# Two attention-decode blocks with their output projections: output weights loaded in rows of 4 KB and 2 KB, head outputs put in that order by selection matmuls

## The chip, the cores and the metric

The kernel runs on one core of one Trainium2 chip. The metric is the device time of one execution in microseconds (us). A core has five engines that run side by side and wait for each other through semaphores: TensorE (PE in the profile, with its weight loads as PEld), VectorE (DVE), ScalarE (ACT), GpSimd (POOL) and SyncE (SP), which here only issues loads. The loads themselves are moved by 16 DMA engines.

## The reference: what is computed

Two attention layers decode one new token for a batch of 4. Each has 32 query heads of 128 elements and a model width of 512. All data is bfloat16.

```python
q = (x @ wq)                                  # [4, 512] @ [512, 4096]
scores = einsum("bhqd,bhkd->bhqk", q, k) * (128 ** -0.5)
p = softmax(scores, axis=-1)
o = einsum("bhqk,bhkd->bhqd", p, v)           # [4, 32, 1, 128]
y = o.reshape(4, 1, 32 * 128) @ wo            # [4, 4096] @ [4096, 512]
```

- Part A, the sliding block: 8 key/value heads, each shared by 4 query heads, and only the last 2048 of 8192 cached positions.
- Part B, the block-cached part: 32 key/value heads and all 8192 positions.

The two results are put side by side: the output is [4, 1, 1024]. Nearly all the data is the caches of part B: 4 x 32 x 8192 x 128 x 2 bytes for the keys and as much for the values, 537 MB of the 587 MB that the kernel reads. The output weights `A_wo` and `B_wo` are 4 MB each.

## The kernel before, in words

**Chunks.** The work is cut into 72 chunks. Chunks 0 to 7 are part A: one key/value head with its 4 query heads for all 4 batch rows, 2 MB of keys and 2 MB of values. Chunks 8 to 71 are part B: one pair of heads and one batch row, 4 MB of keys and 4 MB of values, so four chunks to a pair of heads. A chunk is 64 (A) or 128 (B) tiles of 128 cached positions, handled in groups of 8, numbered g.

**One chunk.** `keys_part` (line 650) runs, for each group g, 8 transposes of key tiles on TensorE (`emit_T`, they land in the PSUM tile `tr`), a copy of the result to SBUF by VectorE or ScalarE (`kt`, lines 437 and 439), and, two groups behind, 8 score matmuls (`emit_S`, PSUM tile `sc`). `values_part` (line 672) runs the value matmuls of the chunk before (`emit_pv`, PSUM tile `po`), between them the last scores of the new chunk, then its maximum and exponential (`stats_rowmax`, `stats_gmax`, `stats_exp`). `norm_sum` makes the sums of the softmax by a matmul with ones, and `norm_out` (line 605) multiplies `po` by their inverse and writes the head outputs, `oT` for part A and `oz` for part B. `emit_fin` (line 618) multiplies head outputs by output weights and adds into one PSUM bank, `fin`, over all chunks.

**The output weights.** `dma_wo(g)` (line 304) loads the 4 heads of a part A group, `dma_wos(hp)` (line 311) the 2 heads of a part B pair. Partition d of the destination takes element d of every head: 4 or 2 separate rows of 512 elements, 1 KB each. The stationary operand of an output matmul is then one head's column of `oT` or `oz`, 128 partitions by 4 batch rows, as `norm_out` left it. Part A makes 4 such matmuls a chunk, part B 2 for every two chunks.

**Order.** Nothing is scheduled by a tool: every engine runs its instructions in the order in which the program adds them (`_Sched.add`), and a wait blocks all that stands behind it on that engine. The calls that matter here stand in `keys_part`:

```python
if 1 <= c < NCA and g == 3:
    stats_exp(c - 1)
if 1 <= c < NCA and g == 6:
    norm_sum(c - 1)
if 2 <= c < NCA and g == 4:
    emit_fin(c - 2)
...
if c >= NCA and c % 2 == 1 and g == 10:
    emit_fin(ahead(c, 2))
```

`finish_A` (line 698) ends part A: for its last chunk it runs statistics, sums, values and output matmuls one after the other. After the last chunk of part B come `norm_sum`, the value matmuls and `emit_fin` (lines 722 to 726).

**Loads.** All big loads are issued by SP in one fixed order (lines 352 to 367). A load waits until its buffer is free: keys until the last transposes of the chunk two before, values until the value matmuls of the chunk two before, output weights of part A until `emit_fin` of the chunk two before, those of part B until the last `emit_fin` of the pair before. SP issues in order, so a load that waits holds back all behind it. `sch.mark` (line 653) marks two-chunk stretches; stretches that repeat become hardware loops on TensorE, VectorE and ScalarE.

Of the kernel before, what the change touches and what calls it, by code (L numbers as in the profile page):

```python
# [19 lines left out]
NSM = 2  # L20
# [2 lines left out]
LASTV = (64, 32, 16, 16)  # L23

TRM0, BC0, L0, Q0, XT0 = 0, 256, 288, 320, 448


class _Record:
# [129 lines left out]
def bass_concat_heads__sliding_block_cached__mha_block_cached__decode_kernel(  # L158
        nc, A_x, A_k, A_v, A_wq, A_wo, B_x, B_k, B_v, B_wq, B_wo, out):
    NB = A_x.shape[0]  # L160
# [4 lines left out]
    DO = A_wo.shape[1]  # L165
    W = min(4096, max(256, SkA // 4))
    REP = HQ // Hkv
# [21 lines left out]
    NC = len(chunks)  # L189
    NCA = Hkv  # L190
# [11 lines left out]
    NONE = -1  # L202
    sch = _Sched()
    with ExitStack() as es:
        block = es.enter_context(nc.Block())

        def sb(name, shape, dt):
            return es.enter_context(nc.sbuf_tensor(name, shape, dt))

        def ps(name, shape, dt):  # L210
            return es.enter_context(nc.psum_tensor(name, shape, dt))
# [26 lines left out]
        oT = sb("oT", [P, NSM, 16], BF16)  # L238
        oz = sb("oz", [P, 8], BF16)
        outsb = sb("outsb", [36, DO], BF16)  # L240
        tr = ps("tr", [P, NTRB, TG * P], BF16)
        sc = ps("sc", [P, 2, 512], F32)
        po = ps("po", [P, 512], F32)
# [30 lines left out]
        sch.add("pool", lambda e: e.memset(pbt[1][:, :, :], 0.0), key=("c_pb", 1))  # L274


        half_of = {}
        held = [[] for _ in range(NH)]
        HALF_A = {"k": (8, 9), "v": (4, 5)}
# [21 lines left out]
        def wo_slot(g):  # L301
            return g % 2 if g < NCA - 1 else 2

        def dma_wo(g):
            src = A_wo[g * 4 * P:(g + 1) * 4 * P, :].rearrange("(hl d) n -> d hl n", d=P)
            slot = wo_slot(g)
            dst = wor[:, slot, :].rearrange("p (hl n) -> p hl n", hl=4)
            sch.add_dma("sp", lambda e: e.dma_start(dst, src), "d_wo%d" % slot,
                        waits=[("fin", g - 2)] if g >= 2 and slot < 2 else [], key=("wo", g))

        def dma_wos(hp):

            src = B_wo[2 * hp * P:2 * (hp + 1) * P, :].rearrange("(hl d) n -> d hl n", d=P)
            sch.add_dma("sp", lambda e: e.dma_start(wos[:, :, :], src), "d_wos",  # L314
                        waits=[("fin", NCA + 4 * hp - 1)] if hp else [], key=("wos", hp))

        def dma_kv(kind, c):
# [51 lines left out]
        ms_read = []  # L369
# [3 lines left out]
        def pe_mm(o, l, r, start=True, stop=True, transpose=False, waits=(), key=None):  # L373
            if transpose:
                sch.add("pe", lambda e: e.transpose(o, l, r), waits, key)  # L375
            else:
                sch.add("pe", lambda e: e.matmul(o, l, r, start=start, stop=stop), waits, key)  # L377
# [229 lines left out]
        def norm_out(c):  # L607
            if 0 <= c < NCA:
                m = c % NSM
                o, i0, i1 = oT[:, m, :], po[:, m * 16:m * 16 + 16], rinv[:, m, :]  # L610
            else:

                o, i0 = oz[:, :].rearrange("p (x y) -> p x y", x=2), bcast(po[:, 0:4], [[0, 2], [1, 4]])
                i1 = rz[:, :].rearrange("p (x y) -> p x y", x=2)
            waits = [("rinv" if 0 <= c < NCA else "rz", c), ("pv", c)] + ([("fin", c - 2 if c != NCA + 1 else NONE)] if c >= 2 else [])
            sch.add("dve", lambda e: e.tensor_tensor(out=o, in0=i0, in1=i1, op=ALU.mult), waits=waits, key=("oT", c))  # L616
            po_read[:] = [("oT", c)]

        def emit_fin(c):
# [103 lines left out]
        for g in range(chunks[NC - 1]["NG"]):  # L723
            emit_pv(NC - 1, g)
        pv_done(NC - 1)
# [60 lines left out]
```

## Time and profile before

| What | Value |
|---|---|
| Median of 3 runs | 1381.89 us (1379.97 to 1385.78) |
| Profiled execution: its own time | 1380.14 us |
| Profiled execution: span of the profile | 1378.3 us |
| TensorE busy | 1174.6 us, 85% of the span |
| VectorE busy | 641.7 us, 47% |
| ScalarE busy | 436.0 us, 32% |
| GpSimd busy | 4.8 us |
| Bytes moved | 587.53 MB, mean 426 GB/s over the span |
| DMA packets | 30085 |
| Output matmuls, part A (`fin<-wor,oT`) | 32 |
| Output matmuls, part B (`fin<-wos,oz`) | 66 |

How to read it: the span is what the profiler saw of one execution, from the first to the last instruction, and the execution's own time is a little longer. The page cuts the span into 40 slices of 34.5 us and gives for each the busy share of every engine and of the 16 DMA engines in tenths, where 9 means 90% or more. A share of busy time says nothing yet of what sets the end: part A fills about the first 125 us of the span, part B the rest, and the two have different limits. A line of the timeline gives start, duration, engine, line and operation, output and inputs, and in brackets how long the engine stood idle before it and what it waited for. The "landing" of a load is the time from its issue on SP until its last byte is there. Loads on one queue land in the order of issue, so the difference between the landing of the load before and the issue of the next is the work that the DMA engines still had in hand.

### The profile page before, as it was taken

How to read it: one execution, taken by the hardware profiler on the slowest of the kernel's cores; microseconds unless marked ns; L12 is line 12 of the kernel's file. 1: busy time of each engine (PE TensorE's matmuls, PEld its weight loads, DVE VectorE, ACT ScalarE, POOL GpSimd, SP SyncE). 2: the span in 40 equal slices, each digit the busy share in tenths (PEclk: the TensorE clock that was granted, in tenths of full speed). 3: DMA queues.
4: the chain of work that ended last, by engine and by line, in shares of the span. 5: the costliest groups of instructions: out<-in, count | busy, mean ns of one | idle time of the engine just before them, and what ended most of it. 6: DMA issues, size and time to landing. Idle time of an engine off the chain costs nothing.

```text
span 1378.3 us, 59408 instructions
## 1 busy us (share of the span) xinstructions
PE 1174.6 (85%) x26901; PEld 1132.8 (82%) x26901; DVE 641.7 (47%) x1337; ACT 436.0 (32%) x649; POOL 4.8 (0%) x18
## 2 busy tenths in 40 slices
PE   4887898888888888888889888988898888888988
PEld 4776898888888887888888888888898888888987
DVE  1665454444444444444444444444454445444543
ACT  1553233323223322332233232322333233332332
POOL 1000000000000000000000000000000000000000
PEclk9999999999999999999999999999999999999998
DMA  9999999999999999999999999999999999999997
GB/s 400 414 417 425 428 432 429 431 432 430 433 430 434 428 432 431 431 432 430 432 429 433 431 432 432 430 430 432 431 431 433 428 433 432 431 431 431 430 431 315
DMA packets 30085, 587.53 MB, mean 426 GB/s; under 512 B 2784, under 2 KB 10992, under 8 KB 11248
## 3 DMA queue, kind: packets, MB, share of 16 engines
q1 hardware_dynamic: 30040, 587.22, 99.6%
q8 instruction: 16, 0.26, 0.1%
q14 instruction: 5, 0.04, 0.0%
q10 hardware_dynamic: 24, 0.01, 0.0%
HBM read 587.21 MB, written 0.01 MB: 426 GB/s over the span
## 4 chain that ended last, share of the span: by engine, by line
DMA 60%; PE 37%; DVE 1%; issue 1%; ACT 0%; SPq 0%; DVEq 0%; ACTq 0%
DMA kv<-in_B_k_cache_dram 58%; PE tr L375 23%; PE sc L377 10%; PE po L377 3%; DMA kv<-in_B_wq_dram 2%; PE fin L377 2%; PE ms L377 1%; DVE sA L488 1%; DVE kt L439 0%; DVE sA L486 0%; ACT pba L551 0%; PE ms L375 0%; SPq L330 0%; SPq L314 0%; ACT kt L437 0%
## 5 line engine op out<-in xcount | busy, mean ns | idle before, releaser
L375 PE MATMUL tr<-identb,kv 128*128 128x128 bf16 x8704 | 703.5, 232 | 160.6 <-DMA kv<-in_B_k_cache_dram 158.2
L439 DVE COPY kt<-tr 128x1024 bf16<-128x1024 bf16 x736 | 503.5, 691 | 469.6 <-PE tr L375 468.6
L375 PEld LDWEIGHTS tr<-identb,kv 128*128 128x128 bf16 x8704 | 559.2, 105 | 185.7 <-DMA kv<-in_B_k_cache_dram 103.5
L437 ACT ACTIVATE kt<-tr 128x1024 bf16<-128x1024 bf16 x352 | 360.2, 1024 | 629.8 <-PE tr L375 628.9
L377 PE MATMUL sc<-qb,kt 128*128 128x64 bf16 x8704 | 446.9, 196 | 10.6 <-DVE kt L439 10.3
L377 PEld LDWEIGHTS sc<-qb,kt 128*128 128x128 bf16 x8704 | 369.3, 100 | 14.5 <-DVE kt L439 11.6
L377 PE MATMUL po<-pbb,kv 128*128 128x64 bf16 (+1 forms) x8320 | 293.8, 191 | 7.0 <-issue 7.0
L377 PEld LDWEIGHTS po<-pbb,kv 128*128 128x128 bf16 x8320 | 266.8, 97 | 9.1 <-issue 7.3
L536 ACT ACTIVATE pbb<-sc,negb 64x128 bf16<-64x128 f32 x128 | 51.2, 400 | 295.2 <-DVE negb L526 294.4
L502 DVE TENSOR_REDUCE rm<-sc 64x1 f32<-64x128 f32 x128 | 37.0, 289 | 93.1 <-PE sc L377 92.2
L514 DVE TENSOR_REDUCE gm<-ms 1x2 f32<-1x128 f32 (+1 forms) x72 | 20.1, 279 | 44.5 <-PE ms L375 44.4
L526 DVE COPY negb<-ms 128x1 f32<-128x1 f32 (+1 forms) x72 | 11.4, 159 | 55.4 <-PE ms L377 55.4
L377 PE MATMUL ms<-identf,gx 1*128 1x1 f32 (+1 forms) x144 | 27.2, 256 | 0.0
L377 PEld LDWEIGHTS ms<-identf,gx 1*128 1x128 f32 (+1 forms) x144 | 21.1, 182 | 4.5 <-DVE gx L518 0.4
L536 ACT ACTIVATION_READ_ACCUMULATOR pbb<-sc,negb 64x1 f32 x128 | 23.7, 185 | 0.0
L375 PE MATMUL ms<-identf,rm 128*1 128x128 f32 (+1 forms) x72 | 19.5, 271 | 2.3 <-DVE rm L497 2.3
L377 PE MATMUL po<-pba,kv 128*128 128x64 bf16 x512 | 20.1, 199 | 0.5 <-ACT pba L551 0.5
L377 PE MATMUL fin<-wos,oz 128*4 128x512 bf16 x66 | 20.0, 385 | 0.3 <-DVE oz L616 0.3
L377 PEld LDWEIGHTS po<-pba,kv 128*128 128x128 bf16 x512 | 17.9, 102 | 0.6 <-ACT pba L551 0.6
L518 DVE TENSOR_SCALAR gx<-gm 1x128 f32<-1x128 f32 (+1 forms) x72 | 15.9, 221 | 2.7 <-DVE gm L514 0.2
L377 PE MATMUL ms<-xT,kv 128*128 128x4 bf16 x256 | 7.1, 166 | 8.5 <-DMA kv<-in_A_wq_dram 4.4
L377 PEld LDWEIGHTS ms<-xT,kv 128*128 128x128 bf16 x256 | 7.0, 104 | 8.7 <-DMA kv<-in_A_wq_dram 4.5
(46 smaller groups left out, 136.0 us busy)
## 6 DMA issues: line engine op xcount, KB each, us to landing
kv<-in_B_k_cache_dram SPq DMA_DIRECT2D x64, 4096.0 KB, 27.3
kv<-in_B_v_cache_dram SPq DMA_DIRECT2D x63, 4096.0 KB, 32.0
kv<-in_A_k_cache_dram SPq DMA_DIRECT2D x8, 2048.0 KB, 14.0
kv<-in_A_v_cache_dram SPq DMA_DIRECT2D x8, 2048.0 KB, 16.2
kv<-in_A_wq_dram SPq DMA_DIRECT2D x1, 4096.0 KB, 12.3
kv<-in_B_wq_dram SPq DMA_DIRECT2D x1, 4096.0 KB, 27.2
wor<-in_A_wo_dram SPq DMA_DIRECT2D x8, 512.0 KB, 11.3
wos<-in_B_wo_dram SPq DMA_DIRECT2D x16, 256.0 KB, 20.8
```

The costliest lines, as they stand in the source:

```text
L375: sch.add("pe", lambda e: e.transpose(o, l, r), waits, key)
L377: sch.add("pe", lambda e: e.matmul(o, l, r, start=start, stop=stop), waits, key)
L437: sch.add("act", lambda e: e.activation(dst, src, ACTF.Copy), waits=waits, key=("ev", s))
L439: sch.add("dve", lambda e: e.tensor_copy(dst, src), waits=waits, key=("ev", s))
L488: emit = lambda e, src=src, b=b: e.scalar_tensor_tensor(out=t, in0=src, scalar=mk[:, b:b + 1], in1=t, op0=ALU.mult, op1=ALU.add)
L502: sch.add("dve", lambda e, src=src, pp=pp: e.tensor_reduce(out=rm[pp, m, 0:1], in_=src, axis=AX.X, op=ALU.max), waits=[("S", ch["s_last"]) ...
L514: sch.add("dve", lambda e: e.tensor_reduce(out=gm[0:C, m, 0:U], in_=src, axis=AX.X, op=ALU.max), waits=[("trm", c)], key=("gmax", c))
L518: sch.add("dve", lambda e: e.tensor_scalar(out=dst, in0=gv, scalar1=-scale, scalar2=None, op0=ALU.mult), waits=[("gmax", c)], key=("gx", c))
L526: sch.add("dve", lambda e: e.tensor_copy(negb[:, m, 0:C], ms[:, col:col + C]), waits=[("bc", c)], key=("negb", c))
L536: sch.add("act", lambda e, src=src, pp=pp, n=n, u=u: e.activation(pbv[pp, :, u], src, ACTF.Exp, bias=negb[pp, m, 0:1], scale=scale, accum_ ...
```

## The change

The rows in which the output weights lie in memory are taken as they come: partition p takes 4 (part A) or 2 (part B) neighbouring rows of the weight matrix, which are one piece of 4 KB or 2 KB. Partition p then no longer holds element p of each head, so the head outputs must be put in the same order before the output matmul. Ten 0/1 matrices made by GpSimd at the start serve for that: `sel4` and `sel2` pick elements, `back2` puts part B weights back in head order.

- `emit_sel(c)` is new: 4 (A) or 2 (B) selection matmuls of a 128x128 0/1 matrix with the head outputs (16 or 8 columns) into the PSUM tile `ms`, then 4 or 2 VectorE copies, each of 32 or 64 partitions, into `zA` or `zB`. `emit_fin` takes its stationary operand from there, and waits for the last copy.
- In `keys_part` of part A, `emit_sel` takes the place of `emit_fin` at g=4, and `emit_fin` moves to g=7. In part B `emit_sel` is added at g=8, and `emit_fin` stays at g=10.
- `norm_out` waits for the selection of the chunk two before and no longer for its output matmuls. What next writes to `ms` (the sums, the maximum) waits for the last copy.
- In `finish_A`, `emit_sel(NCA - 2)` is added after the maximum, `emit_fin(NCA - 2)` moves behind `stats_exp`, and `emit_sel(NCA - 1)` stands between the values and the last output matmuls of part A.
- For the last two chunks of part B the weights are put back in head order instead: `emit_wol` adds 4 matmuls of 512 columns and two copies (ScalarE and VectorE) between the last `norm_sum` and the last value matmuls.
- The matmul that clears `fin` waits for the 0/1 matrices.

```diff
+        for r in range(4):
+            sch.add("pool", lambda e, r=r: e.affine_select(
+                out=sel4[:, r, :], in_=onesb[:, :], pattern=[[0, 4], [-4, 32]], compare_op=ALU.is_equal,
+                fill=0.0, base=-r, channel_multiplier=1), waits=["c_onesb"])
...
         def dma_wo(g):
-            src = A_wo[g * 4 * P:(g + 1) * 4 * P, :].rearrange("(hl d) n -> d hl n", d=P)
+            src = A_wo[g * 4 * P:(g + 1) * 4 * P, :].rearrange("(p r) n -> p (r n)", r=4)
...
         def dma_wos(hp):
-            src = B_wo[2 * hp * P:2 * (hp + 1) * P, :].rearrange("(hl d) n -> d hl n", d=P)
+            src = B_wo[2 * hp * P:2 * (hp + 1) * P, :].rearrange("(p r) n -> p (r n)", r=2)
...
-            waits = [("rinv" if 0 <= c < NCA else "rz", c), ("pv", c)] + ([("fin", c - 2 if c != NCA + 1 else NONE)] if c >= 2 else [])
+            waits = [("rinv" if 0 <= c < NCA else "rz", c), ("pv", c)] + ([("sm", c - 2 if c != NCA + 1 else NONE)] if c >= 2 else [])
...
+        def emit_sel(c):
+            if 0 <= c < NCA:
+                sel, x, n, z, k = sel4, oT[:, c % NSM, :], 16, zA[:, c % 2, :], 4
+                free = [("fin", c - 2)] if c >= 2 else []
+            else:
+                sel, x, n, z, k = sel2, oz[:, :], 8, zB[:, :], 2
+                free = [("fin", c - 2 if c - 2 >= NCA else NONE)] if c != NONE else []
+            for r in range(k):
+                pe_mm(ms[:, Z0 + r * n:Z0 + (r + 1) * n], sel[:, r, :], x,
+                      waits=[("oT", c)] + ms_read if r == 0 else [], key=("sm", c) if r == k - 1 else None)
+            for h in range(k):
+                pp = slice(h * P // k, (h + 1) * P // k)
+                src = ms[pp, Z0:Z0 + k * n].rearrange("p (r b h) -> p h r b", r=k, b=NB)[:, h]
+                sch.add("dve", lambda e, src=src, pp=pp: e.tensor_copy(z[pp, :].rearrange("p (r b) -> p r b", r=k), src),
+                        waits=[("sm", c)] + free if h == 0 else [], key=("z", c) if h == k - 1 else None)
+            ms_read[:] = [("z", c)]
+
+        def emit_wol():
+            for u in range(2):
+                o = tr[:, u, :].bitcast(F32)
+                for r in range(2):
+                    pe_mm(o, back2[:, u, r, :], wos[:, r, :], start=r == 0, stop=r == 1,
+                          waits=[("wos2", NC - 1)] if u == r == 0 else [], key=("back", u) if r else None)
+                if u == 0:
+                    sch.add("act", lambda e, o=o: e.activation(wol[:, 0, :], o, ACTF.Copy), waits=[("back", 0)], key=("wol", 0))
+                else:
+                    sch.add("dve", lambda e, o=o: e.tensor_copy(wol[:, 1, :], o), waits=[("back", 1)], key=("wol", 1))
...
-            if ab == 1:
+            if c == NC - 1:
                 ov = oz[:, :].rearrange("p (b u) -> p b u", u=2)
-                ops = [(ov[:, :, u], wos[:, u, :]) for u in range(2)]
-                waits = [("oT", c), ("wos2", c)]
+                ops = [(ov[:, :, u], wol[:, u, :]) for u in range(2)]
+                waits = [("oT", c), ("wol", 0), ("wol", 1)]
+            elif ab == 1:
+                ops = [(zB[:, r * NB:(r + 1) * NB], wos[:, r, :]) for r in range(2)]
+                waits = [("z", c), ("wos2", c)]
             else:
-                w = wor[:, wo_slot(c), :].rearrange("p (hl n) -> p hl n", hl=4)
-                ov = oT[:, c % NSM, :].rearrange("p (u c) -> p u c", c=REP)
-                ops = [(ov[:, :, cc], w[:, cc, :]) for cc in range(REP)]
-                waits = [("oT", c), ("wo", c)]
+                w = wor[:, wo_slot(c), :].rearrange("p (r n) -> p r n", r=4)
+                ops = [(zA[:, c % 2, r * NB:(r + 1) * NB], w[:, r, :]) for r in range(4)]
+                waits = [("z", c), ("wo", c)]
...
                 if 2 <= c < NCA and g == 4:
+                    emit_sel(c - 2)
+                if 2 <= c < NCA and g == 7:
                     emit_fin(c - 2)
...
+                if c >= NCA and c % 2 == 1 and g == 8:
+                    emit_sel(ahead(c, 2))
                 if c >= NCA and c % 2 == 1 and g == 10:
                     emit_fin(ahead(c, 2))
...
         def finish_A():
             stats_gmax(NCA - 1)
+            emit_sel(NCA - 2)
+            stats_exp(NCA - 1)
             emit_fin(NCA - 2)
-            stats_exp(NCA - 1)
             norm_sum(NCA - 1)
             for g in range(chunks[NCA - 1]["NG"]):
                 emit_pv(NCA - 1, g)
             pv_done(NCA - 1)
+            emit_sel(NCA - 1)
             emit_fin(NCA - 1)
...
-                pe_mm(fin[0:36, :], pbt[0][:, 1, 0:36], pbt[0][:, 1, 0:DO], stop=False, waits=[("c_pb", 1)])
+                pe_mm(fin[0:36, :], pbt[0][:, 1, 0:36], pbt[0][:, 1, 0:DO], stop=False, waits=["c_sel"])
...
         norm_sum(NC - 1)
+        emit_wol()
         for g in range(chunks[NC - 1]["NG"]):
             emit_pv(NC - 1, g)
```

More of the change, by code (lines that the diff above doesn't have):

```diff
@@ L25 @@
 TRM0, BC0, L0, Q0, XT0 = 0, 256, 288, 320, 448
+Z0 = Q0
 class _Record:
@@ L240, in bass_concat_heads__sliding_block_cached__mha_block_cached__decode_kernel @@
         outsb = sb("outsb", [36, DO], BF16)
+        sel4 = sb("sel4", [P, 4, P], BF16)
+        sel2 = sb("sel2", [P, 2, P], BF16)
+        back2 = sb("back2", [P, 2, 2, P], BF16)
+        zA = sb("zA", [P, 2, 16], BF16)
+        zB = sb("zB", [P, 8], BF16)
+        wol = sb("wol", [P, 2, DO], BF16)
         tr = ps("tr", [P, NTRB, TG * P], BF16)
@@ L274, in bass_concat_heads__sliding_block_cached__mha_block_cached__decode_kernel @@
         sch.add("pool", lambda e: e.memset(pbt[1][:, :, :], 0.0), key=("c_pb", 1))
+        for r in range(4):
[3 more added lines that the diff above has]
+        for r in range(2):
+            sch.add("pool", lambda e, r=r: e.affine_select(
+                out=sel2[:, r, :], in_=onesb[:, :], pattern=[[0, 2], [-2, 64]], compare_op=ALU.is_equal,
+                fill=0.0, base=-r, channel_multiplier=1))
+            for u in range(2):
+                sch.add("pool", lambda e, r=r, u=u: e.affine_select(
+                    out=back2[:, u, r, :], in_=onesb[:, :], pattern=[[1, P]], compare_op=ALU.is_equal,
+                    fill=0.0, base=P * u - r, channel_multiplier=-2), key="c_sel" if r == u == 1 else None)
         half_of = {}
@@ L304, in dma_wo @@
         def dma_wo(g):
-            src = A_wo[g * 4 * P:(g + 1) * 4 * P, :].rearrange("(hl d) n -> d hl n", d=P)
+            src = A_wo[g * 4 * P:(g + 1) * 4 * P, :].rearrange("(p r) n -> p (r n)", r=4)
             slot = wo_slot(g)
-            dst = wor[:, slot, :].rearrange("p (hl n) -> p hl n", hl=4)
+            dst = wor[:, slot, :]
             sch.add_dma("sp", lambda e: e.dma_start(dst, src), "d_wo%d" % slot,
@@ L311, in dma_wos @@
         def dma_wos(hp):
-            src = B_wo[2 * hp * P:2 * (hp + 1) * P, :].rearrange("(hl d) n -> d hl n", d=P)
-            sch.add_dma("sp", lambda e: e.dma_start(wos[:, :, :], src), "d_wos",
+            src = B_wo[2 * hp * P:2 * (hp + 1) * P, :].rearrange("(p r) n -> p (r n)", r=2)
+            sch.add_dma("sp", lambda e: e.dma_start(wos[:, :, :].rearrange("p r n -> p (r n)"), src), "d_wos",
                         waits=[("fin", NCA + 4 * hp - 1)] if hp else [], key=("wos", hp))
@@ L614, in norm_out @@
                 i1 = rz[:, :].rearrange("p (x y) -> p x y", x=2)
-            waits = [("rinv" if 0 <= c < NCA else "rz", c), ("pv", c)] + ([("fin", c - 2 if c != NCA + 1 else NONE)] if c >= 2 else [])
+            waits = [("rinv" if 0 <= c < NCA else "rz", c), ("pv", c)] + ([("sm", c - 2 if c != NCA + 1 else NONE)] if c >= 2 else [])
             sch.add("dve", lambda e: e.tensor_tensor(out=o, in0=i0, in1=i1, op=ALU.mult), waits=waits, key=("oT", c))
             po_read[:] = [("oT", c)]
+        def emit_sel(c):
[15 more added lines that the diff above has]
+        def emit_wol():
+            for u in range(2):
+                o = tr[:, u, :].bitcast(F32)
+                for r in range(2):
+                    pe_mm(o, back2[:, u, r, :], wos[:, r, :], start=r == 0, stop=r == 1,
[4 more added lines that the diff above has]
+                    sch.add("dve", lambda e, o=o: e.tensor_copy(wol[:, 1, :], o), waits=[("back", 1)], key=("wol", 1))
         def emit_fin(c):
```

## The prediction

> **What bounds the kernel now.** I read the page's slices and chain first, then the waits, then each load's landing, then the timeline of one sliding-block chunk and of the end.
>
> ```profile
> DMA  9999999999999999999999999999999999999997
> DMA packets 30085, 587.53 MB, mean 426 GB/s; under 512 B 2784, under 2 KB 10992, under 8 KB 11248
> DMA 60%; PE 37%; DVE 1%; issue 1%; ACT 0%; SPq 0%; DVEq 0%; ACTq 0%
> wor<-in_A_wo_dram SPq DMA_DIRECT2D x8, 512.0 KB, 11.3
> wos<-in_B_wo_dram SPq DMA_DIRECT2D x16, 256.0 KB, 20.8
> ```
>
> The 16 DMA engines are busy in every slice. 8192 of the packets are the 1 KB rows of the output weights. In the waits of all engines, TensorE stands still mostly for keys of the block-cached part:
>
> ```profile
> PE tr L375 <- DMA kv<-in_B_k_cache_dram: 158.2, 59, 4.5
> PE po L377 <- issue: 7.0, 3, 3.2
> ```
>
> So that part, from about 225 us on, runs at the pace of the transfers, with 158.2/59 = 2.7 us of slack for TensorE per chunk. The sliding-block part does not: its chain of waits between 36 and 104 us holds only TensorE, VectorE and ScalarE pieces. One of its chunks, from the timeline:
>
> ```profile
> 107.02 1.03 PE L377 MATMUL fin<-wor,oT 128*4 128x512 bf16 x4
> 107.45 1.71 ACT L551 ACTIVATE pba<-eA,mk 128x256 bf16<-128x256 bf16 x4
> 107.98 0.62 PE L375 MATMUL tr<-identb,kv 128*128 128x128 bf16 x8
> 108.00 0.69 DVE L439 COPY kt<-tr 128x1024 bf16<-128x1024 bf16 x1
> 109.06 2.17 ACT L437 ACTIVATE kt<-tr 128x1024 bf16<-128x1024 bf16 x2
> 110.12 0.41 PE L377 MATMUL sc<-qb,kt 128*128 128x64 bf16 x8
> 110.36 0.86 PE L377 MATMUL po<-pba,kv 128*128 128x64 bf16 x24
> 112.40 0.48 DVE L486 TENSOR_SCALAR sA<-sc,mk 128x256 f32<-128x256 f32 x1 [2.24 <-PE sc L377]
> ```
>
> The scores at 110.12 wait for ScalarE's first copy (109.06 + 1.02), which is behind the four copies of the probabilities. The output matmuls at 107.02 lie inside that wait. What covers a late load is the queue: the landing of each load, asked around its issue, e.g. of the last sliding-block value load:
>
> ```profile
> L330 SPq DMA_DIRECT2D kv<-in_A_v_cache_dram x1: 541/541/541, 101.7 to 101.7; - x1
> ...
> DMA to landing us min/median/max: 11.5/11.5/11.5
> ```
>
> It lands at 113.2, 4.9 us behind the load before it (108.3). So when it was issued (101.72) the queue still held 6.6 us of work. By the same reading the next loads found 12.4 us (issue 123.20), 10.2 (135.95), 10.7 (145.12), 8.0 (157.56), 9.2 (166.04), 7.1 (177.88), 11.8 (182.85), 10.7 (193.73), and 14 to 23 from 209 on.
>
> **What the Trainium skill says.** "DMA: Bandwidth & Descriptors", section Why small descriptors are slow (HBM only): each packet carries a fixed overhead of about 3 cycles beside its 32-byte beats; its Specifications name 512 B as the least size for line rate. The trace agrees that 1 KB rows are nearly at rate: 46 ns each (below). The same page, Anatomy of one DMA, gives about 2.0 us of fixed cost per DMA (on GpSimd's path); here the last output DMA, issued at 1376.53 on SP, ends by 1378.3, 1.8 us. I use 2.0 us for a load that finds the queue empty. "Runtime: NRT & Kernel Launch", section Instruction fetch mechanics: TensorE holds 2048 instructions, fetched in blocks of 256. The built loop bodies grow from 818 to 838 and from 1594 to 1599 instructions, so both still fit; the trace shows 16 fetched packets in all, 0.26 MB, no refetching.
>
> **The change part by part.**
>
> *Rows of the weights.* Each DMA engine takes 1/16. A 4 MB load lands 9.72 us behind the last one: 8 packets of 32 KB, 1215 ns each. A sliding-block weight load lands 1.45 us after (32 packets of 1 KB, 45 ns), a block-cached one 0.74 (16, 46 ns). The line through 1 KB and 32 KB is 37.7 ns per KB + 8.3 ns per packet. So 4 KB costs 159 ns and 2 KB 84 ns: a sliding-block load 8 x 159 = 1.27 against 32 x 46 = 1.47 us, -0.20; a block-cached one 8 x 84 = 0.67 against 0.74, -0.07. In all 8 x 0.20 + 16 x 0.07 = 2.7 us. Bounds: 0 if the cost goes by bytes. At most the whole excess: landings of successive keys are 39.63 us apart with a weight load between them and 38.83 without, so 0.80 where 0.61 is the full rate, 0.19 x 16 = 3.0; a sliding-block trio takes 11.33 where 10.93 is the rate, 0.40 x 8 = 3.2; together 6.2.
>
> *Sliding-block output matmuls, from g=4 to g=7.* Selection takes their place at g=4: 4 matmuls with 16 columns, at 28 ns (the 128 projection matmuls take 3.57 us in the chain) 0.11 us, inside ScalarE's wait. VectorE then makes four 32-partition copies behind the copy at 108.00: 0.17 us each by the oT row, or 0.08 where such small ones overlap, so 0.35 to 0.68, ended by 109.05 to 109.4; the sum matmul (at 109.34) now waits for them, and behind it the transposes at 109.56; 0 to 0.3 us, I take 0. The output matmuls now stand behind the scores of 110.12, with nothing beside them: their 0.96 us (107.02 to 107.98) push the value matmuls and all that follows. Six chunks: 5.8 us. SP also waits longer: the weight load waits for these matmuls, and the next keys are queued behind it, about 1.7 us later beside the slip.
>
> *Between the parts.* The last sliding-block chunk runs alone (lines 698 to 706). Its output matmuls (123.50) now follow 4 selections and 4 copies: at the halved clock there 0.3 + 0.5 + two handoffs of about 0.2 = 1.2 us (0.8 to 1.6). So the block-cached chunks start at about 132 and not at 125.3, 6.7 us late, although their keys have landed.
>
> *What the queue makes of it.* I shift the issues by the slips, subtract 0.20 per weight load, and let a load land no sooner than 2.0 us + its own length after issue. The last sliding-block value load (+4.8) finds 0.4 us of queue: that eats the 1.4 us saved so far, and it lands at 113.4. The first block-cached keys land at 125.05 (125.17). The load of 135.95 finds 2 to 3 us of queue, that of 157.56 (now 164.2) less than 1, so it lands at 164.2 + 2.0 + 9.7 = 175.9 (175.3 before); that of 177.88 (184.5) finds 1.1 and lands at 196.3 (194.7). From there five more loads of 9.72 to 9.77 us, the weights and the keys of 225.24 follow without a gap: these keys land at 255.4 and not 253.7, +1.7, and TensorE has caught up (it needs them at 252.7). Each us of slip beyond about 5 costs one.
>
> *Block-cached chunks.* Two selections (0.06 us) and two 64-partition copies (0.16 to 0.33 us) per two chunks of 39 us: covered by the 2.7 us of key wait; outputs stay at g=10, two groups (1.4 us) after selection. Without that cover 32 x 0.4 = 13 us. The 14 weight loads that remain save 14 x 0.07 = 0.9 us.
>
> *The end.* From the last keys (1352.35) TensorE is the chain, and it does not wait for the last values:
>
> ```profile
> 1370.82 0.38 PE ms L377 x2
> 1371.20 3.26 PE po L377 x128
> 1374.77 1.03 PE fin L377 x2
> ```
>
> The four 512-column matmuls that put the last weights back in order stand between the first two: 4 x 0.22 = 0.9 us (0.52 per pair at line 377), plus 0.1 for one selection. Their copies (0.68 us, as outsb) lie beside the 3.26 us. +1.0 (0.85 to 1.3).
>
> GpSimd's ten selects (0.29 each) end near 8.7 us, and the first user is at 32.7: nothing.
>
> **Sum.** +1.7 - 0.9 + 1.0 = +1.8 us. On the profiled execution's own 1380.14 us (span 1378.3, 1.84 around it) that is 1381.9; on the median 1381.89 it is 1383.7. I take 1382.8.
>
> **Rivals.**
> 1. *Output matmuls stay covered* (or the queue absorbs all): -2.7 + 1.0 = -1.7, about 1379; with the full 6.2, 1375.5. For: 6.6 us of queue at its lowest. Against: nothing runs beside them at g=7.
> 2. *Slower: the queue runs dry between the parts.* If a sliding-block chunk loses 1.8 us rather than 0.96, since the sum matmul and transposes also wait for VectorE's copies (0.3) and the key copies behind them (0.5), the slip is 10.8 + 1.2 = 12, 5.3 more than above: +7.1, 1388 to 1391. It decides from 1.75 us per chunk. For: VectorE is what the chunk waits for elsewhere (rows at 108.00, 112.40). Against: those copies have about 0.4 us of room.
> 3. *Rows cut to 1 KB again, or cost by bytes*: saves nothing, +2.7, about 1384.5.
> 4. *Instruction fetch* (the three "issue" stalls, 7.0 us, in the first pass of the block-cached loop) falls elsewhere: -3 to +4 on the slip.
>
> **Chances.** Forecast 0.52, rival 1 0.17, rival 2 0.19, rivals 3 and 4 0.12. A measurement of this kernel tells about 0.5%, 6.9 us, from no change. Faster by more needs the full saving, no slip and no end cost: 0.05. Slower by more: rival 2 and part of 4, 0.21. Same: 0.74. The range runs from rival 1 with half the full saving (1377) into rival 2 (1390).
>
> **What would show it.** Packets under 2 KB fall from 10992 to 2800. A sliding-block chunk takes 12.1 us between value loads, not 11.2. The first block-cached transposes start near 132, well after their keys land. Loads between 100 and 180 us find under 3 us of queue. Weight loads land about 1.27 and 0.67 us after the load before. From 260 us on a period of two chunks lasts 39.2 us as before, less some hundredths. The last value matmuls start 0.9 us later after their probabilities. It is wrong if the sliding-block chunks keep 11.2 us, if key waits in the block-cached part vanish, or if TensorE waits there for selection copies.

## The result, and the profile after

| | before | after |
|---|---|---|
| Median of 6 runs each | 1380.51 us (1379.87 to 1385.78) | 1386.25 us (1384.81 to 1387.83) |
| Ratio after/before | | 1.0035, 95% interval 1.0019 to 1.0052 |
| Span of the profiled execution | 1378.3 us | 1386.1 us |
| Last keys have landed | 1352.35 us | 1358.23 us |
| From there to the end of the span | 25.95 us | 27.87 us |
| First block-cached transposes | 125.29 us | 133.40 us |

The changed kernel is slower by 0.35% (4.8 us by the ratio, 5.7 by the medians). The forecast was +1.8. The loss is less than the 0.5% that the prediction took as the least a measurement can tell; the interval nevertheless excludes 1. The two spans differ by 7.8 us, since the profiled execution of after (1387.83) is the slowest of its six: 2 to 3 us of what its trace shows belong to this execution and not to the median. What follows first explains the spans, then tests by medians. Part A is the sliding-block part, part B the block-cached one.

The rate in 40 slices, first of before (34.5 us each), then of after (34.7 us), with the lines of the page of after that answer to those shown of before:

```profile
GB/s 400 414 417 425 428 432 429 431 432 430 433 430 434 428 432 431 431 432 430 432 429 433 431 432 432 430 430 432 431 431 433 428 433 432 431 431 431 430 431 315
```

```profile
GB/s 400 423 389 410 371 435 427 431 436 431 429 430 434 430 430 435 431 431 429 433 431 433 429 432 434 431 429 430 435 431 428 435 430 429 430 435 431 428 431 292
DMA packets 24965, 587.53 MB, mean 424 GB/s; under 512 B 2784, under 2 KB 2800, under 8 KB 6128
...
DMA 59%; PE 36%; DVE 3%; issue 1%; ACT 1%; DVEq 0%; SPq 0%; ACTq 0%
...
wor<-in_A_wo_dram SPq DMA_DIRECT2D x8, 512.0 KB, 5.6
```

The change does what it says: 8192 packets of 1 KB have become 3072 larger ones. But slices 3 to 5 (69 to 173 us) now move 389, 410 and 371 GB/s, where before had 417, 425 and 428, and from slice 6 on the rate is the old one. A part A weight load lands 5.6 us after its issue and no longer 11.3: 0.2 us of that is its shorter transfer, the rest is queue that is no longer there. The waits of after:

```profile
PE tr L399 <- DMA kv<-in_B_k_cache_dram: 159.1, 59, 4.4
...
DVE zB L657 <- PE ms L401: 8.4, 32, 0.3
...
PE po L401 <- issue: 5.2, 2, 4.1
```

TensorE's wait for part B keys is as before (158.2 then), and nobody in part B waits long for a selection. So part B runs as it did, only later.

**A chunk of part A.** The timeline of after, to be read beside the one in the prediction:

```profile
113.17 0.25 PE L401 MATMUL ms<-oT,sel 128*128 128x16 bf16 x4
...
113.68 1.70 ACT L575 ACTIVATE pba<-eA,mk 128x256 bf16<-128x256 bf16 x4
...
114.84 0.71 DVE L657 CAST zA<-ms 32x16 bf16<-32x16 f32 x4
...
115.61 0.40 PE L401 MATMUL ms<-rsa,onesf 128*128 128x16 f32 x2 [0.22 <-DVE zA L657]
...
116.35 0.41 PE L401 MATMUL sc<-qb,kt 128*128 128x64 bf16 x8
...
116.69 1.02 PE L401 MATMUL fin<-wor,zA 128*4 128x512 bf16 x4
117.64 0.87 PE L401 MATMUL po<-pba,kv 128*128 128x64 bf16 x24
```

The selection takes 0.25 us inside ScalarE's work at 113.68. The output matmuls (116.69) stand behind the scores, and the values follow at once (117.64): 0.95 us with nothing beside it. The times between value loads are 12.54, 12.67, 12.32, 12.22 and 12.28 us; before they were 11.16 to 11.26.

**Where the 7.8 us arose.** For the loads that matter, the issue on SP, the queue found (landing of the load before, minus the issue) and the landing:

| Load | before: issue, found, lands | after: issue, found, lands | later by |
|---|---|---|---|
| last A keys | 87.81, 9.2, 101.9 | 93.61, 3.8, 104.3 | 2.4 |
| last A values | 101.72, 6.6, 113.2 | 107.95, 2.5, 116.7 | 3.5 |
| first B keys | 104.09, 11.4, 125.2 | 109.65, 9.0, 128.4 | 3.2 |
| B values | 123.20, 13.0, 146.1 | 131.05, 7.4, 148.0 | 1.9 |
| B keys | 135.95, 10.2, 155.8 | 144.23, 3.7, 159.7 | 3.9 |
| B values | 145.12, 10.7, 165.6 | 155.35, 4.4, 170.2 | 4.7 |
| B keys ("K") | 157.56, 8.0, 175.3 | 167.96, 2.3, 182.5 | 7.2 |
| B keys, 225 us | 225.24, 18.8, 253.7 | 232.51, 18.6, 260.9 | 7.2 |

(The first B keys are followed at once by a second load of keys, which before received 11.1 us after them and after 10.1; therefore the B values are only 1.9 us later.) All of the loss stands by 182.5 us. From there to the last keys after gains 1.3 us (7.2 - 5.9 = 14 weight loads x 0.09), and the tail costs 1.9: 7.2 - 1.3 + 1.9 = 7.8.

The load K of after, from the answer for the buffer that it fills:

```profile
L366 SPq DMA_DIRECT2D kv<-in_B_k_cache_dram x1: 328/328/328, 168.0 to 168.0; - x1
...
DMA to landing us min/median/max: 14.5/14.5/14.5
```

It found 2.3 us of work in the queue and needs 9.72 for itself: 12.0. It took 14.5.

### The profile page after: what moved, and what is told of

It reads as the page before. It is cut to its first block, busy times and chain, and to the rows that moved or that the text cites. A ratio compares the mean times of both kernels' runs of the same rounds, so it can differ in the third digit from the quotient of the medians.

```text
span 1386.1 us, 59796 instructions
## 1 busy us (share of the span) xinstructions
PE 1178.7 (85%) x27001; PEld 1134.9 (82%) x27001; DVE 657.1 (47%) x1434; ACT 436.6 (31%) x650; POOL 7.4 (1%) x28
## 4 chain that ended last, share of the span: by engine, by line
DMA 59%; PE 36%; DVE 3%; issue 1%; ACT 1%; DVEq 0%; SPq 0%; ACTq 0%
DMA kv<-in_B_k_cache_dram 57%; PE tr L399 21%; PE sc L401 9%; PE po L401 2%; DMA kv<-in_B_wq_dram 2%; PE fin L401 2%; PE ms L401 1%; DVE sA L512 1%; DVE kt L463 0%; DVE zA L657 0%; DVE sA L510 0%; ACT pba L575 0%; DVE sA L568 0%; ACT eA L572 0%; DVE rs L579 0%
## 5 line engine op out<-in xcount | busy, mean ns | idle before, releaser
L399 PE MATMUL tr<-identb,kv 128*128 128x128 bf16 x8704 | 700.0, 231 | 162.3 <-DMA kv<-in_B_k_cache_dram 159.1
L399 PEld LDWEIGHTS tr<-identb,kv 128*128 128x128 bf16 x8704 | 555.5, 104 | 184.3 <-DMA kv<-in_B_k_cache_dram 101.9
L401 PE MATMUL sc<-qb,kt 128*128 128x64 bf16 x8704 | 449.5, 197 | 12.6 <-DVE kt L463 12.3
L550 DVE COPY negb<-ms 128x1 f32<-128x1 f32 (+1 forms) x72 | 11.4, 159 | 54.1 <-PE ms L401 54.1
L401 PE MATMUL fin<-wos,zB 128*4 128x512 bf16 x64 | 19.0, 378 | 0.0
L510 DVE TENSOR_SCALAR sA<-sc,mk 128x256 f32<-128x256 f32 x8 | 3.9, 484 | 23.5 <-PE sc L401 23.5
L657 DVE CAST zB<-ms 64x8 bf16<-64x8 f32 x64 | 10.5, 164 | 8.9 <-PE ms L401 8.4
## 6 DMA issues: line engine op xcount, KB each, us to landing
kv<-in_A_wq_dram SPq DMA_DIRECT2D x1, 4096.0 KB, 12.2
```

The lines of the kernel that those rows point to most:

```text
L510: emit = lambda e, src=src: e.tensor_scalar(out=t, in0=src, scalar1=mk[:, 0:1], scalar2=None, op0=ALU.mult)
L550: sch.add("dve", lambda e: e.tensor_copy(negb[:, m, 0:C], ms[:, col:col + C]), waits=[("bc", c)], key=("negb", c))
L657: sch.add("dve", lambda e, src=src, pp=pp: e.tensor_copy(z[pp, :].rearrange("p (r b) -> p r b", r=k), src), waits=[("sm", c)] + free if h ...
```

## The experiments

The first four were compared with before on one chip (1380.64 us, median of 26 runs), the next four on another occasion (1380.96, 47 runs), the last two on a third (1380.90, 35 runs). Times are medians, ratios are to before with their 95% interval.

### The later output matmuls alone

```diff
-                if 2 <= c < NCA and g == 4:
+                if 2 <= c < NCA and g == 7:
                     emit_fin(c - 2)
```

This is before with one digit changed: old rows, no selection.

> The kernel before with one edit: the output matmuls of the sliding-block part stand at g=7 and not at g=4. No new rows, no selection. Theory (their new place is exposed, and the late loads then find the queue nearly empty): a sliding-block chunk takes 12.1 us between value loads in place of 11.2, the first block-cached transposes start near 131 us (125.3 before), the keys issued at 157.6 before are issued near 163.5 and land 4.8 us plus their own length later, about 178 (175.3 before): 2 to 5 us slower, about 1383.5. Rival (the queue absorbs a late issue, and the loss of the change comes from the selection work): no slower than before by more than 1 us.

Measured: 1385.33 us, ratio 1.0034 (1.0021 to 1.0046). The first B transposes start at 132.79 us, the last keys land at 1359.87. Its chunk, in the timeline:

```profile
115.03 0.43 PE L377 MATMUL sc<-qb,kt 128*128 128x64 bf16 x8
...
116.29 1.03 PE L377 MATMUL fin<-wor,oT 128*4 128x512 bf16 x4
117.25 0.87 PE L377 MATMUL po<-pba,kv 128*128 128x64 bf16 x24
```

The same order as in after (scores, output matmuls, values), and chunks of 12.2 to 12.3 us. Its load K is issued at 167.88, finds 2.1 us and lands at 182.7, as in after. One digit gives a loss as large as that of the whole change. (That the two are equal is a balance. The next two runs show that the new rows give back about 2 us, and that the order with all its selections costs 0.18% more than the late output matmuls alone, though there the two intervals overlap.) Since the chunks are as long as those of after, which have the selection copies too, these copies cost nothing within a chunk.

### The rows alone, and the order alone

```diff
-            src = A_wo[g * 4 * P:(g + 1) * 4 * P, :].rearrange("(hl d) n -> d hl n", d=P)
+            src = A_wo[g * 4 * P:(g + 1) * 4 * P, :].rearrange("(p r) n -> p (r n)", r=4)
...
-            src = B_wo[2 * hp * P:2 * (hp + 1) * P, :].rearrange("(hl d) n -> d hl n", d=P)
+            src = B_wo[2 * hp * P:2 * (hp + 1) * P, :].rearrange("(p r) n -> p (r n)", r=2)
```

The first is before with these two lines, the second is after without them. So in both the weights and the head outputs stand in different orders: the first leaves out the selection, the second the new rows.

> The kernel before with the new rows of both output weights and nothing else; the head outputs are not put in the order of the rows, so the projection is left wrong. Theory: 8 loads save 0.2 us and 16 save 0.1 us on a queue that never runs empty: 3.2 us faster, about 1377.3, and the first block-cached transposes start where they did. Rival (the new rows are not cheaper, or slow the loads around them): within 1 us of before, or slower.

> The changed kernel with the weights loaded in the old 1 KB rows; the selection then puts the head outputs in an order that the weights do not have, so the projection is left wrong. Theory: all of the loss is here; the savings of the sliding-block loads are eaten by the empty queue anyway, so only the 15 later block-cached loads are missed, 1.4 us more than the changed kernel: 6 to 7.5 us slower than before, about 1387. Rival (the rows are what slows it): faster than the changed kernel, near before.

Measured: rows alone 1378.70 us, 0.9990 (0.9982 to 0.9998), last keys at 1348.98; order alone 1388.05 us, 1.0052 (1.0039 to 1.0066), last keys at 1359.87. The rows are worth 3.4 us at the last keys (forecast: 8 x 0.20 + 16 x 0.07 = 2.7), of which 1.4 to 1.9 reach the time here; between order alone and after they are worth 0.17%, 2.3 us. So larger rows are a gain, and the reordering takes more than it.

### Part A put back

```diff
-            src = A_wo[g * 4 * P:(g + 1) * 4 * P, :].rearrange("(p r) n -> p (r n)", r=4)
+            src = A_wo[g * 4 * P:(g + 1) * 4 * P, :].rearrange("(hl d) n -> d hl n", d=P)
...
                 if 2 <= c < NCA and g == 4:
-                    emit_sel(c - 2)
-                if 2 <= c < NCA and g == 7:
                     emit_fin(c - 2)
```

This is after with the loads, the order and the end of part A as before; part B keeps its rows, its selections and its end.

> The changed kernel with its sliding-block part as before (1 KB rows, output matmuls at g=4 on the head outputs themselves); rows, selection and the end of the block-cached part as changed. Theory (the loss is the sliding-block part): 16 block-cached loads save 1.6 us, the end costs 0.9: 0.7 us faster than before, about 1379.8. Rival (the selections and copies of the block-cached part delay TensorE or VectorE): as slow as the changed kernel within 2 us, 1384 or more.

Measured: 1379.91 us, 0.9998 (0.9983 to 1.0012). The last keys land 1.39 us earlier than before (16 x 0.09), the tail is 0.99 longer, and TensorE's key wait is 156.1 us. The selections of part B are free, its rows save about what its end costs, and the loss lies in part A.

### Half of the output matmuls late

```diff
                 if 2 <= c < NCA and g == 4:
-                    emit_fin(c - 2)
+                    emit_fin(c - 2, 0)
+                if 2 <= c < NCA and g == 7:
+                    emit_fin(c - 2, 1)
```

Before again, with two of the four matmuls at g=4 and two at g=7. It asks whether the cost has a threshold.

> The kernel before with only two of the four output matmuls of each sliding-block chunk at g=7, the other two at g=4. Half the slip: about 0.5 us a chunk, the last sliding-block values issued near 104.4 us (101.7 before, 107.2 with all four late). Theory (a load that lands some 15 us after its issue at the earliest, so slip costs only beyond what the queue still holds): the queue still covers nearly all of it, at most 1.5 us slower than before, under a third of what all four cost. Rival (each us of slip costs the same from the first): half of the 4.7 us, 2.4 us slower or more.

Measured: 1382.49 us, 1.0007 (0.9997 to 1.0016). Part B starts 3.4 us late (128.65) and the last keys land 1.07 us late. With all four late it was 7.5 and 7.5 us. So in the two traces the first 3.4 us of slip cost 1.1, the next 4.1 cost 6.4. By the times the second price is lower: half costs 1.0 to 1.5 us and all four 4.7, so the next 4.1 us cost 3.2 to 3.7. (The profiled execution of late_fin_only is the slowest of its six, that of half_late is faster than its median.) The cost is far from even, which speaks for a threshold, though the interval of half_late reaches 2.2 us, nearly half of 4.7; that the price beyond it is more than one to one is not shown. Two loads show where it lies: here K found 3.8 us and landed 10.5 us after the load before it, 0.8 more than its own 9.72; the keys after that found 4.8 us and landed 9.71 after.

### The cover restored in part A

```diff
                 if 2 <= c < NCA and g == 4:
                     emit_sel(c - 2)
-                if 1 <= c < NCA and g == 6:
-                    norm_sum(c - 1)
-                if 2 <= c < NCA and g == 7:
+                if 1 <= c < NCA and g == 4:
+                    stats_rows(c - 1)
+                if 2 <= c < NCA and g == 6:
                     emit_fin(c - 2)
+                if 1 <= c < NCA and g == 6:
+                    norm_sum(c - 1)
```

After, with the selection copies ahead of VectorE's row sums and the output matmuls ahead of the sum matmul. (`stats_rows` is the part of `stats_exp` that makes the row sums; only its place is new.)

> The changed kernel with the selection kept, but VectorE's selection copies put ahead of the row sums of the exponential, and the output matmuls of the sliding-block part at g=6 ahead of the sum matmul, where ScalarE is still at its copies. Theory: a sliding-block chunk takes 11.2 to 11.4 us again, the first block-cached transposes start near 127 us (the serial end of the sliding-block part still has its two selections, 1.6 us), the rows' saving of 3 us comes through to the last keys, and the end costs its 0.9: about 2 us faster than before, 1378.5. Rival (the selection itself is what costs): 1384 or more.

Measured: 1381.82 us, 0.9999 (0.9989 to 1.0009). In its timeline the output matmuls are back inside ScalarE's four copies:

```profile
84.87 1.71 ACT L575 ACTIVATE pba<-eA,mk 128x256 bf16<-128x256 bf16 x4
...
85.90 1.02 PE L401 MATMUL fin<-wor,zA 128*4 128x512 bf16 x4
```

Four of the five measured chunks take 11.2 us again and the loss is gone. The fifth took 12.75 us; TensorE's granted clock was 0.50 in it from 95 to 98 us. A gain over before was expected too and did not come: the last keys land at 1352.77, and not 3 us earlier. Part B still starts 2.1 us late (127.42), of which that chunk is 1.5; the loads of 139.71, 149.10 and 161.57 find 4.2, 5.0 and 2.6 us of queue, and the last of them lands 11.4 us after the one before instead of 9.72. The time that the rows save shortens the queue as well: where it is thin, the saving is paid back. So it is at this load, which lands 0.3 us later than K of before. Another 1.4 us go where no queue was thin: two loads of keys (443.7 and 1325.2) that found 15.6 and 17.1 us landed 0.7 us late each. All this is one trace; no run separates these parts.

### The end

```diff
-        norm_sum(NC - 1)
         emit_wol()
+        norm_sum(NC - 1)
         for g in range(chunks[NC - 1]["NG"]):
             emit_pv(NC - 1, g)
```

After, with the last weights put in order before the last sum matmul, which waits for ScalarE.

> The changed kernel with the four matmuls that put the last weights back in order ahead of the last sum matmul, where TensorE waits 0.86 us for the exponential. Theory: the last value matmuls follow the sum matmul at once again, 0.8 to 0.9 us faster than the changed kernel, about 1385.4. Rival (the copies of the reordered weights, not the matmuls, are what is late): no gain.

Measured: 1384.94 us, 1.0026 (1.0016 to 1.0036). The end in the timeline, first of after, then of this kernel:

```profile
1377.72 0.39 PE L401 MATMUL ms<-rsb,onesf 128*128 128x4 f32 x2 [0.86 <-ACT pbb L560]
1377.97 1.02 PE L401 MATMUL tr<-wos,back 128*128 128x512 bf16 x4
1378.83 3.43 PE L401 MATMUL po<-pbb,kv 128*128 128x2 bf16 x128
```

```profile
1373.98 0.39 PE L401 MATMUL ms<-rsb,onesf 128*128 128x4 f32 x2
1374.23 3.38 PE L401 MATMUL po<-pbb,kv 128*128 128x2 bf16 x128
```

In after the values start 1.11 us behind the sum matmul, here 0.25: the 0.86 us has gone into the wait for the probabilities. The time falls by 0.09%, 1.2 us, but the two intervals overlap, so that the gain in time is likely and not secured.

### Combinations

Three kernels join these edits. The first has the restored cover, the early reorder and one edit more, which puts the selection in `finish_A` behind `stats_exp`:

```diff
             stats_gmax(NCA - 1)
-            emit_sel(NCA - 2)
             stats_exp(NCA - 1)
+            emit_sel(NCA - 2)
+            stats_rows(NCA - 1)
             emit_fin(NCA - 2)
```

> Both mends together, and in the serial end of the sliding-block part the selection stands behind the matmul that spreads the maximum. Theory: faster than before by the rows' saving alone, 3 us less the last selection of the sliding-block part which the queue covers: about 1377.6, and no dearer end than before. Rival: the rows' saving does not reach the end, same as before within 1 us.

Measured: 1382.18 us, 1.0013 (1.0003 to 1.0024). The expected gain is not there. The timeline shows what took it in the profiled execution, at the start of part B:

```profile
133.67 2.63 PE L399 MATMUL tr<-identb,kv 128*128 128x128 bf16 x23 [5.01 <-issue]
```

TensorE stood 5.01 us with nothing that the profile shows to wait for. The next keys were then issued 2.4 us after the queue had run empty.

The second is the first without that edit, the third is the kernel with part A put back plus the early reorder.

> The kernel of cover_restored with the last weights' reordering ahead of the last sum matmul; the serial end of the sliding-block part as in cover_restored. Theory (what kept cover_and_early from gaining is the 5.0 us stand of TensorE, waiting for nothing the profile shows, ahead of the first block-cached transposes, and not the moved reordering): that stand is absent again, the last keys land as in cover_restored (about 1352.8 in the profile) and the end is 0.9 us shorter: 0.5 to 1.5 us faster than before, about 1379.8. Rival (the moved reordering is what costs): as slow as cover_and_early, 1382 or more.

> The kernel of part_a_undone (2 KB rows and selection in the block-cached part alone, sliding-block part as before) with the last weights' reordering ahead of the last sum matmul. Theory: 16 loads save 0.09 us each and nothing is added to the path: last keys 1.4 us earlier than before, end as before, 1.4 us faster, about 1379.5. Rival (the selections of the block-cached part cost at the end as well): no faster than before.

Measured: 1379.23 us, 0.9989 (0.9978 to 1.0000), and 1379.34 us, 0.9990 (0.9984 to 0.9997). Both are 1.4 to 1.7 us faster than before; the third is the simpler and the better secured, while the interval of the second reaches 1. The second has no stall ahead of the first transposes, as expected. Its profiled execution took 1386.01 us, the longest of its fourteen: TensorE had half its clock for 3.4 us in each of three chunks of part A (from 62.5, 86.4 and 110.3 us), and they took 12.7 us. So its trace says little of its median.

## Why the prediction was off, step by step

Its mechanism was the right one: covered matmuls become exposed in part A, loads are issued later, the queue runs thin between the parts, the fuller queue further on hides the rest, and the end adds a little. The measured 1386.25 us lies within its range, but the forecast gave +1.8 where the measurement gave +4.8; that the range held owes something to luck, since it was the second rival that stretched it upward, and by another way than the one found. The sum fell short in the first term, "what the queue makes of it": +1.7 forecast, +7.2 in the trace. Part of this is the slow execution: in the trace of early_reorder, the same kernel up to its end, load K lands 6.0 us later than in before. (One reading of the prediction was off, though nothing hung on it: the load of 123.20 found 13.0 us and not 12.4.)

- **Rows: right, a little low.** Weight loads of part A land 1.22 to 1.29 us after the load before (forecast 1.27), but for two that met a thin queue (2.0 and 2.2); those of part B land 0.62 to 0.68 after it (forecast 0.67), where before had 0.69 to 0.74. So a part B load is 0.06 shorter, near the 0.07 forecast; at the last keys each is worth 0.09.
- **Output matmuls at g=7: right.** 0.96 us a chunk forecast; the last three of the five measured chunks lost 1.06. The first two lost 1.4 and 1.5 (in the second the trace shows TensorE at half its clock from 63 to 67 us). So the last A values are issued 6.2 us late, and not 4.8.
- **VectorE's selection copies in a chunk: right at nothing.** They take 0.71 us (0.35 to 0.68 forecast); TensorE waits 0.22 for them, and late_fin_only loses as much without them.
- **Serial end: right sum, wrong place.** From the issue of the last A values to part B's start the kernel lost 25.45 - 23.57 = 1.9 us, as forecast, of which 1.06 is the last chunk. The prediction charged 1.2 to the selection of the last chunk. In the trace of after:

```profile
122.43 0.27 PE L399 MATMUL ms<-identf,rm 128*4 128x128 f32 x1 [2.29 <-DVE rm L521]
...
124.14 0.38 PE L401 MATMUL ms<-identf,gx 4*128 4x4 f32 x2 [0.81 <-DVE zA L657]
...
132.45 1.02 PE L401 MATMUL fin<-wor,zA 128*4 128x512 bf16 x4 [0.81 <-DVE zA L657]
133.40 1.51 PE L399 MATMUL tr<-identb,kv 128*128 128x128 bf16 x24
```

  The broadcast of the maximum (124.14) writes to `ms` and so waits 0.81 us for the copies of the selection added just ahead of it, a wait that the prediction left out: from the maximum's transpose to the end of the broadcast it is 2.09 us where before had 1.53. The selection of the last chunk takes 1.08 us itself (0.27 and the wait of 0.81 at 132.45), near the 1.2 charged, but adds only about 0.3: the values end at 131.02 and the transposes start 2.38 us later, where before it was 2.12, since there the output matmuls ran at half the clock (1.52 against 1.02 us) and the keys still took 0.26.
- **"A load lands no sooner than 2.0 us plus its own length after issue": this failed.** The price came from the last output DMA (1.8 us) and from the Trainium skill, "DMA: Bandwidth & Descriptors", Anatomy of one DMA (about 2.0 us per DMA). Neither is a 2 or 4 MB load behind others. Landing minus issue minus own length, for the five loads of the table above that found less than 5 us in after: last A keys 10.7 - 4.9 = 5.8, last A values 3.9, then 15.5 - 9.7 = 5.8, 5.1 and 4.8 us. A load that finds less queue than this leaves a gap. The same holds in all twelve traces: of the 22 key and value loads of part B that found 5.3 us or less, 21 landed 0.36 us or more later than their length after the load before (3.3 at most, and 6.2 where the queue had run empty); they needed 3.8 to 6.2 us beyond their length. Those that found more lost 0.7 us at most, but for the second load of keys, which lost up to 1.7 with 17 us or more in the queue, for a reason not looked for. With 4.8 instead of 2.0 for K and for the load issued at 184.5, the forecast's own sum grows by 2.7 us (199.0 instead of 196.3 for the second).
- **K's issue: 164.2 forecast, 167.96 measured.** 1.4 us of these 3.8 are the later start of part B. Another 2.3 arise between that start and the issue (32.27 us before, 34.56 after): 1.4 in stalls of TensorE named "issue", most of the rest in matmuls behind the longer stall, where TensorE had half its clock for 6.8 us and in before for 3.4. The stalls in the timeline, first before, then after:

```profile
137.69 0.74 PE L377 MATMUL po<-pbb,kv 128*128 128x64 bf16 x20 [1.42 <-issue]
...
144.07 0.37 PE L377 MATMUL po<-pbb,kv 128*128 128x64 bf16 x7 [2.45 <-issue]
...
164.39 0.80 PE L377 MATMUL po<-pbb,kv 128*128 128x64 bf16 x22 [3.18 <-issue]
```

```profile
145.71 0.74 PE L401 MATMUL po<-pbb,kv 128*128 128x64 bf16 x20 [1.16 <-issue]
...
153.73 0.53 PE L401 MATMUL po<-pbb,kv 128*128 128x64 bf16 x7 [4.09 <-issue]
```

  Ahead of K's issue these are 5.25 us; before had 1.42 and 2.45 there, and its third (3.18) fell behind the issue, where the next load still found 9.2 us of queue. That was rival 4, priced at up to 4 us but kept out of the forecast. late_fin_only has the same pair (1.48 and 3.82) with exactly the instructions of before, so the added instructions are not the reason.

  The traces also tell what TensorE waits for there. The page of before and that of after have this line among the DMA queues:

```profile
q8 instruction: 16, 0.26, 0.1%
```

  These are 16 packets of 16 KB each, and the trace has the time of every one. The first stall of before ends at 137.69, 1.3 us after such a packet (135.26 to 136.35), the second at 144.07, 1.2 us after the next (141.72 to 142.83); the 4.09 us of after end 1.4 us after that of 151.39 to 152.35. So it is with all 34 "issue" stalls over 0.25 us in the twelve traces: each ends 1.2 to 1.7 us after one of these packets. And those within part B stand 256 instructions apart or a multiple of it, to within one: the stalls that end at 137.69, 144.07 and 164.39 come 508, 764 and 1532 matmuls and weight loads behind its first transpose. (The stall of 5.01 us, ahead of the first transposes, is not within it.)
- **"Each us of slip beyond about 5 costs one": the start of the cost was wrong.** half_late and late_fin_only together put it between 2 and 3 us of slip (an estimate: 3.4 less 1.1 us at the price beyond). That price is 1.6 per us in their two traces but 0.8 to 0.9 by their times, so one per us is not refuted.
- **Part B and the end: right.** The key wait is 159.1 us. The reorder stands in the chain with 0.88 us (0.9 forecast). The tail's other 1.0 is mainly a slower clock under the first transposes of the last keys (2.74 us for 24 of them, 1.90 before), which I take for chance of the execution: kernels with one and the same end differ as much (24.4 us in early_reorder and 26.9 in the first combination; 25.9 in before and 26.8 in rows_only).

Of the rivals, the second had the price of the first term (+7.1) and the dry queue, but not the way to it: its point of decision was a loss of 1.75 us per chunk, and the chunks lost 1.06 to 1.5. The first and the third are excluded by late_fin_only and by the landings of the weights.

**What stays open.** Why a load needs 4 to 6 us beyond its length when the queue is thin was not tried by itself. The packets in the trace of after show parts of it. The 16 DMA engines do not end a load together: each load ends with sixteen packets of 4 bytes, and for the load ahead of K these end between 167.20 and 169.73 us. So at 168.0, when K has just been issued, only 8 packets of 32 KB are under way, where a full queue has 16, although the queue found still counts 2.3 us. The 16 packets of 32 KB that start between 168 and 170 us take 1.9 us on average, and not 1.2. No run tried how much each of these is worth.

The prediction argued for the "issue" stalls with the Trainium skill, "Runtime: NRT & Kernel Launch", Instruction fetch mechanics, where TensorE's instructions come in blocks of 256. The traces agree: the stalls stand at such distances and end behind a packet of that queue. So they are waits for instructions, in the first pass of part B's loop (one of 0.30 us in part A apart), from 0.3 to 5.0 us long. Why such a packet comes late is open: in after the one behind the long stall starts 1.75 us after TensorE has stopped, in before 0.1 us after.

## What to carry to other kernels

Before moving a small operation out of a cover, follow the delay to the next load's issue and ask how much work the DMA queue still holds there (landing of the load before, minus the issue). In these traces the delay was free as long as some 5 us remained; below that the load came later, by about 5 us minus what it found. Saving transfer time thins the same queue, so such a gain has to be paired with loads that are issued no later. A latency measured on a small, lone transfer did not hold here for a large one behind others; take it from a load of the same kind that met a short queue.

## What the runs showed of the hardware

The busy share of the DMA engines hardly shows a thin queue. One stretch around K's landing, first before, then after; the last two columns are the DMA share and GB/s:

```profile
165.00:175.00 10.00, 10.00 (x189) 9.93 (x186) 5.83 (x12) 3.98 (x7) 0.00 (x0) 0.83 1.00 430
```

```profile
165.00:175.00 10.00, 10.00 (x270) 9.86 (x268) 4.72 (x11) 3.69 (x7) 0.00 (x0) 1.00 0.89 339
```

The share falls by a tenth, the rate by a fifth; between 145 and 150 us it is 0.85 at 269 GB/s, where before has 1.02 at 436. The share counts the longer packets of this stretch (those of 168 to 170 us above) as busy time, and so the page's row of nines for DMA hides them; its row of GB/s doesn't.
